# The first layer's high part of the weights times both parts of x in one product of 512 columns, from chunk 3 on

## The chip, the cores and the metric

The kernel runs on one core of a Trainium2 chip. The metric is the device time of one execution in microseconds (us). Engines are named as in the profile: PE multiplies matrices, PEld is its loading of the stationary operand, DVE is the vector engine, ACT the scalar engine, POOL the general engine, SP issues most transfers.

## The reference

Attention over 4 batches of 8 heads (768 positions, 64 wide) with a window of 128 positions and 4 sink positions, and then a feed-forward layer with a leaky activation on the 3072 resulting rows of width 512.

```python
scores = scale * np.matmul(q, k.transpose(0, 1, 3, 2))
keep = is_sink | in_window                      # 4 sinks, 128 positions back
a = softmax(np.where(keep, scores, -1e9))
x = np.matmul(a, v)                             # -> (3072, 512)
h = x @ w_in                                    # 512 -> 2048
g = np.maximum(h, 0.0) + alpha * np.minimum(h, 0.0)
out = g @ w_out                                 # 2048 -> 512, float32
```

## The kernel before

The 3072 rows are worked on in 12 chunks of 256 rows (`QC`), and the hidden width of 2048 in 16 blocks of 128 (`f`). PE multiplies in a reduced format, so a full product is made of three: each operand is split into a high part and the rest, and high x high, high x low and low x high are added up in PSUM. W_in and W_out of a block lie split in `fins[f]`, x of a chunk in `xh` and `xl` (a 128 x 4 x 256 tile each, two buffers each), and g in `gh` and `gl`.

A block (c, f) is `gemm1` and, two blocks later (`LAG`), `gemm2`. `gemm1` makes 12 products of 256 columns into one bank of the kind "h" (two such banks): for each of the four 128-row slices `kt` of x the high weights times `xh`, the high weights times `xl`, and the low weights times `xh` (L961). ACT then scales the bank by alpha into g (L977), DVE takes the larger of bank and g (L978), ACT rounds g to `gh` (L979), and DVE subtracts to get `gl` (L980). `gemm2` makes six products of 512 columns with them (L1034 and L1035 with `gh`, L1032 with `gl`) into the chunk's two output banks.

Beside the blocks of chunk c runs the attention of chunk c + 1: 16 units (8 heads, two halves of the queries). A unit is two score products on PE (L639, L640) into one of two banks of the kind "s", a masked sum with a maximum on DVE (L652), an exponential on ACT (L656), and scaling and combining on DVE (L686, L687, L698). For each pair of heads the weights are transposed through two transfers and masked on DVE (L780, L798 to L803). At the end `av_four` multiplies them by the values (L901, L914, L909), ACT rounds the result to `xh` (L946) and DVE subtracts to get `xl` (L947). Only then can the next chunk's first block start. Preparing a head's operands takes two DVE instructions (L605, L607); a further one (L441) looks through the weights for unusual exponents, in four blocks of a chunk.

Which step of the attention goes with which block is written down: the steps are spread over the first `SPAN` blocks of a chunk, and `av_four` goes with a later one:

```python
*most, last = attention(c + 1)
work += spread(most, SPAN) + [[] for _ in range(NF - SPAN)]
work[-3].append(last)
```

That order is only the rank of each operation. A list scheduler (`Plan.draw`) goes through all operations with a table of costs, takes for each engine the one that can start first (the lower rank among those nearly as early), and emits each engine's instructions in the order found; a set of nudges (`NUDGES`) moves the rank of some operations of chunks 0 to 2. What an engine's queue holds is therefore fixed before the run.

Of the kernel before, what the change touches and what calls it, by code (L numbers as in the profile page):

```python
# [48 lines left out]
SPAN = 12  # L49
# [23 lines left out]
WHOLE = 2  # L73
FIRST = 4
# [250 lines left out]
def cast(n, psum=False):  # L325
    return (0.045 if psum else 0.092) + 0.84e-3 * n
# [18 lines left out]
def mm(n):  # L345
    return 0.456e-3 * n
# [12 lines left out]
def program(ctx, tc, qk, qs, pairs, vp, vw, vq, vs, w, par, out):  # L359
# [33 lines left out]
    several("xh", 2, [P, KT, QC], F32R)  # L393
    several("xl", 2, [P, KT, QC], F32R)
# [194 lines left out]
    xh, xl, prep, comb, sink, ptile_, sums, rinv, nms, wt = {}, {}, {}, {}, {}, {}, {}, {}, {}, {}  # L589
# [233 lines left out]
    def begin_x(c, p):  # L823
        if p == 0:
            xh[c], xl[c] = val("xh"), val("xl")
        return xh[c], xl[c]

    def av_two(c, g):
# [11 lines left out]
        x1, x2 = begin_x(c, 2 * g)  # L840
        part = slice(2 * g, 2 * g + 2)
        keys = [[(t, x) for x in both] for t in (x1, x2)]
        view = lambda: bk.at.rearrange("p (n x) -> p n x", n=2)
        op("ACT", cast(4 * P, True), lambda: nc.scalar.copy(x1.at[:, part], view()), reads=[bk], writes=keys[0])
# [3 lines left out]
        op("DVE", dve(4 * P), lambda: nc.vector.tensor_tensor(x2.at[:, part], view(), x1.at[:, part].bitcast(F32), ALU.subtract),  # L848
           reads=[bk, *keys[0]], writes=keys[1])

    def av_split(c, g):
# [24 lines left out]
        x1, x2 = begin_x(c, 2 * g)  # L876
        part = slice(2 * g, 2 * g + 2)
        keys = [(x1, x) for x in both], [(x2, x) for x in both]
# [7 lines left out]
        op("ACT", cast(4 * P), lambda: nc.scalar.copy(x1.at[:, part], view()), reads=xs, writes=keys[0])  # L886
# [3 lines left out]
        op("DVE", dve(4 * P), lambda: nc.vector.tensor_tensor(x2.at[:, part], view(), x1.at[:, part].bitcast(F32), ALU.subtract),  # L890
           reads=[*xs, *keys[0]], writes=keys[1])

    def av_four(c):
# [11 lines left out]
        x1, x2 = begin_x(c, 0)  # L905
# [36 lines left out]
        for n, bk in enumerate(bks):  # L942
            part = slice(2 * n, 2 * n + 2)
            keys = [[(t, x) for x in range(2 * n, 2 * n + 2)] for t in (x1, x2)]
            view = lambda bk=bk: bk.at.rearrange("p (n x) -> p n x", n=2)
            op("ACT", cast(4 * P, True), lambda part=part, view=view: nc.scalar.copy(x1.at[:, part], view()), reads=[bk], writes=keys[0])  # L946
            op("DVE", dve(4 * P), lambda part=part, view=view: nc.vector.tensor_tensor(x2.at[:, part], view(), x1.at[:, part].bitcast(F32), ALU.subtract),  # L947
               reads=[bk, *keys[0]], writes=keys[1])
# [5 lines left out]
    def gemm1(c, f):  # L954
        bk, fin, x1, x2 = val("s" if c == NCHUNK - 1 and f >= NF - 2 else "h"), fins[f], xh[c], xl[c]
        h = lambda: bk.at[:, :QC]

        def some(kt):
            ks = slice(kt * P, (kt + 1) * P)
            for n, (part, rhs) in enumerate(((0, x1), (0, x2), (1, x1))):  # L960
                nc.tensor.matmul(h(), fin.at[:, 0, part, ks], rhs.at[:, kt], start=(kt == 0 and n == 0), stop=(kt == KT - 1 and n == 2))  # L961
# [12 lines left out]
        for kt in range(KT):  # L974
            op("PE", 3 * mm(QC), lambda kt=kt: some(kt), reads=[fin, (x1, kt), (x2, kt)], writes=[bk], tail=R_TAIL)
# [422 lines left out]
```

## Time and profile before

| | before |
|---|---|
| time, median of 3 runs | 655.55 us (655.27 to 655.95) |
| span of the profiled execution, first to last instruction | 653.5 us |
| PE busy | 646.0 us, 99% of the span |
| weight loads (PEld) busy | 577.5 us, 88% |
| DVE busy | 528.1 us, 81% |
| ACT busy | 387.0 us, 59% |
| granted PE clock | full in every slice |

The page of the profile gives the span of the profiled execution and not its whole time; the timed runs lie 1.8 to 2.4 us above that span, which is what comes before the first and after the last instruction. Busy time counts an instruction from its start to its end, and neighbours on one engine overlap: what an instruction takes away from its engine is read from start to start.

### The profile page before, as it was taken

How to read it: one execution, taken by the hardware profiler on the slowest of the kernel's cores; microseconds unless marked ns; L12 is line 12 of the kernel's file. 1: busy time of each engine (PE TensorE's matmuls, PEld its weight loads, DVE VectorE, ACT ScalarE, POOL GpSimd, SP SyncE). 2: the span in 40 equal slices, each digit the busy share in tenths (PEclk: the TensorE clock that was granted, in tenths of full speed). 3: DMA queues.
4: the chain of work that ended last, by engine and by line, in shares of the span. 5: the costliest groups of instructions: out<-in, count | busy, mean ns of one | idle time of the engine just before them, and what ended most of it. 6: DMA issues, size and time to landing. Idle time of an engine off the chain costs nothing.

```text
span 653.5 us, 14186 instructions
## 1 busy us (share of the span) xinstructions
PE 646.0 (99%) x4966; PEld 577.5 (88%) x4966; DVE 528.1 (81%) x1708; ACT 387.0 (59%) x1036; POOL 43.6 (7%) x139
## 2 busy tenths in 40 slices
PE   8999999999999999999999999999999999999997
PEld 4678988899999999999999999999999998998996
DVE  7999999987869959968968987986985995996332
ACT  6999667566456547638637736636645753753332
POOL 4100000010000001000000100001000000100000
PEclk9999999999999999999999999999999999999999
DMA  9996203743634646564563654574573564551001
GB/s 338 403 347 259 74 13 109 233 146 112 186 118 131 211 141 198 163 191 146 192 197 111 197 175 149 167 226 130 153 227 111 163 201 152 152 152 53 33 1 37
DMA packets 66508, 106.19 MB, mean 162 GB/s; under 512 B 10241, under 2 KB 33281, under 8 KB 66433
## 3 DMA queue, kind: packets, MB, share of 16 engines
q1 hardware_dynamic: 66144, 104.72, 49.7%
q8 instruction: 40, 0.66, 0.4%
q10 hardware_dynamic: 288, 0.53, 0.3%
q14 instruction: 36, 0.29, 0.2%
HBM read 87.14 MB, written 18.09 MB: 161 GB/s over the span
## 4 chain that ended last, share of the span: by engine, by line
PE 96%; ACT 1%; DVE 1%; DMA 0%; issue 0%; POOL 0%; SPq 0%; DVEq 0%
PE bank L961 40%; PE bank L1032 13%; PE bank L1034 13%; PE bank L1035 13%; PE bank L909 3%; PE bank L640 3%; PE bank L639 3%; PE bank L914 2%; PE bank L818 1%; PE bank L630 1%; PE bank L901 1%; ACT pt L656 1%; PE bank L965 1%; PE bank L994 1%; PE bank L677 0%; DMA param<-par 0%
## 5 line engine op out<-in xcount | busy, mean ns | idle before, releaser
L961 PE MATMUL bank<-xh,w 128*128 128x256 f32 x1520 | 300.5, 281 | 0.3 <-DVE g L978 0.2
L961 PEld LDWEIGHTS bank<-xh,w 128*128 128x128 f32 x1520 | 246.6, 189 | 5.7 <-DVE g L978 1.0
L961 PE MATMUL bank<-xl,w 128*128 128x256 f32 x760 | 212.3, 279 | 0.0
L1034 PE MATMUL bank<-w,gh 128*128 128x512 f32 (+1 forms) x390 | 150.3, 387 | 0.0
L977 ACT ACTIVATE g<-bank,param 128x256 f32<-128x256 f32 x190 | 89.6, 472 | 101.3 <-PE bank L961 93.7
L1035 PE MATMUL bank<-w,gh 128*128 128x512 f32 (+1 forms) x390 | 148.7, 385 | 0.0
L961 PEld LDWEIGHTS bank<-xl,w 128*128 128x128 f32 x760 | 143.3, 189 | 4.3
L979 ACT CAST gh<-g 128x256 fp32r<-128x256 f32 x190 | 77.2, 406 | 76.8 <-DVE g L978 75.9
L656 ACT ACTIVATE pt<-pt,nm 128x260 f32<-128x260 f32 (+1 forms) x192 | 94.5, 493 | 43.9 <-DVE nm L652 41.1
L978 DVE TENSOR_TENSOR g<-bank,g 128x256 f32<-128x256 f32 x190 | 79.6, 420 | 48.9 <-ACT g L977 47.1
L1032 PE MATMUL bank<-w,gl 128*128 128x512 f32 (+1 forms) x390 | 118.3, 388 | 0.0
L980 DVE TENSOR_TENSOR gl<-g,gh 128x256 fp32r<-128x256 f32 x190 | 79.5, 419 | 22.2 <-ACT gh L979 20.1
L652 DVE CUSTOM_DVE_ANT_0 pt<-bank,masks 128x260 f32<-128x260 f32 (+1 forms) x192 | 75.2, 401 | 14.4 <-PE bank L640 12.1
L1032 PEld LDWEIGHTS bank<-w,gl 128*128 128x128 f32 x390 | 70.7, 188 | 14.1 <-DVE gl L980 0.2
L1034 PEld LDWEIGHTS bank<-w,gh 128*128 128x128 f32 x390 | 73.4, 188 | 8.4
L1035 PEld LDWEIGHTS bank<-w,gh 128*128 128x128 f32 x390 | 73.4, 188 | 8.4
L702 POOL TENSOR_TENSOR sink<-pt,ri 128x8 f32<-128x8 f32 x80 | 23.7, 300 | 381.3 <-DVE ri L687 285.7
L605 DVE TENSOR_TENSOR kq<-stage,kq 64x392 fp32r<-64x392 f32 x80 | 45.1, 564 | 3.1
L640 PE MATMUL bank<-kq 128*128 128x260 f32 (+1 forms) x160 | 44.6, 281 | 0.0
L603 ACT CAST kq<-stage 128x392 fp32r<-128x392 f32 x80 | 41.1, 514 | 4.7 <-PE bank L640 3.4
L639 PE MATMUL bank<-kq 128*128 128x260 f32 (+1 forms) x160 | 43.7, 276 | 0.0
L698 DVE CUSTOM_DVE_ANT_0 comb<-pt,ri 128x128 f32<-128x128 f32 x136 | 43.2, 346 | 0.5
(141 smaller groups left out, 705.4 us busy)
## 6 DMA issues: line engine op xcount, KB each, us to landing
stage<-qs SPq DMA_DIRECT2D x80, 324.0 KB, 3.0
wraw<-w SPq DMA_DIRECT2D x16, 1024.0 KB, 9.0
wa<-w SPq DMA_DIRECT2D x32, 512.0 KB, 4.7
v<-vq SPq DMA_DIRECT2D x40, 256.0 KB, 3.7
swap<-comb SPq DMA_DIRECT2D x40, 256.0 KB, 2.2
comb<-swap SPq DMA_DIRECT2D x40, 256.0 KB, 3.4
out_dram<-ob SPq DMA_DIRECT2D x22, 256.0 KB, 3.5
stage<-pairs SPq DMA_DIRECT2D x4, 324.0 KB, 8.7
```

Of the source, the lines that this page charges most:

```text
L639: nc.tensor.matmul(s[:, w0], qh()[:, qs], ks()[:, kw], start=True, stop=False)
L640: nc.tensor.matmul(s[:, w0], ql()[:, qs], ks()[:, kw], start=False, stop=True)
L652: op("DVE", dve(n), lambda: nc.vector.tensor_tensor_reduce(out=pt.at[:, u, w0], in0=s.at[:, w0], in1=masks[:, i, w0], scale=-0.125, scalar ...
L656: op("ACT", exp(n), lambda: nc.scalar.activation(pt.at[:, u, w0], pt.at[:, u, w0], AF.Exp, bias=nm.at[:, h, u:u + 1], scale=-1.0, accum_ou ...
L961: nc.tensor.matmul(h(), fin.at[:, 0, part, ks], rhs.at[:, kt], start=(kt == 0 and n == 0), stop=(kt == KT - 1 and n == 2))
L977: op("ACT", act(QC, True), lambda: nc.scalar.activation(g.at, h(), AF.Copy, scale=alt[:, f:f + 1]), reads=[bk, known("param")], writes=[g])
L978: op("DVE", dve(QC), lambda: nc.vector.tensor_tensor(g.at, h(), g.at, ALU.max), reads=[bk], writes=[g])
L979: op("ACT", cast(QC), lambda: nc.scalar.copy(gh.at, g.at), reads=[g], writes=[gh])
L980: ending.append(op("DVE", dve(QC), lambda: nc.vector.tensor_tensor(gl.at, g.at, gh.at.bitcast(F32), ALU.subtract), reads=[g, gh], writes=[ ...
L1032: nc.tensor.matmul(to, gl.at[:, js], fin.at[:, 1, 0, cs], start=False, stop=(f == NF - 1))
L1034: nc.tensor.matmul(to, gh.at[:, js], fin.at[:, 1, 0, cs], start=(f == 0), stop=False)
L1035: nc.tensor.matmul(to, gh.at[:, js], fin.at[:, 1, 1, cs], start=False, stop=False)
```

## The change

From chunk 3 (`WIDE`) on, the high weights of a slice meet `xh` and `xl` in one product of 512 columns: the two parts of x lie in one tile, and the product fills the whole bank, its left half with high x high and its right half with high x low. The third product (low weights times the high part of x, 256 columns) is added to the left half. ACT then copies the right half to g instead of scaling the bank, DVE adds the left half to it, and a second DVE instruction multiplies by alpha and takes the larger value. So a block has 8 products instead of 12, as many columns as before, and one DVE instruction more. The attention's steps are spread over 11 blocks instead of 12, and `av_four` is ranked one block earlier. The edits of `av_two`, `av_split` and `av_four` only name the two parts of the one tile.

```diff
-SPAN = 12
+SPAN = 11
...
+WIDE = 3
...
-    several("xh", 2, [P, KT, QC], F32R)
-    several("xl", 2, [P, KT, QC], F32R)
+    several("x", 2, [P, 2, KT, QC], F32R)
...
     def begin_x(c, p):
         if p == 0:
-            xh[c], xl[c] = val("xh"), val("xl")
-        return xh[c], xl[c]
+            xs_of[c] = val("x")
+        return xs_of[c]
+
+    def x_keys(x, heads):
+        return [[(x, (n, h)) for h in heads] for n in range(2)]
...
     def gemm1(c, f):
-        bk, fin, x1, x2 = val("s" if c == NCHUNK - 1 and f >= NF - 2 else "h"), fins[f], xh[c], xl[c]
+        bk, fin, xx = val("s" if c == NCHUNK - 1 and f >= NF - 2 else "h"), fins[f], xs_of[c]
         h = lambda: bk.at[:, :QC]
+        wide = c >= WIDE
 
         def some(kt):
             ks = slice(kt * P, (kt + 1) * P)
-            for n, (part, rhs) in enumerate(((0, x1), (0, x2), (1, x1))):
-                nc.tensor.matmul(h(), fin.at[:, 0, part, ks], rhs.at[:, kt], start=(kt == 0 and n == 0), stop=(kt == KT - 1 and n == 2))
+            if wide:
+                nc.tensor.matmul(bk.at, fin.at[:, 0, 0, ks], xx.at[:, :, kt], start=kt == 0, stop=False)
+            else:
+                for n in range(2):
+                    nc.tensor.matmul(h(), fin.at[:, 0, 0, ks], xx.at[:, n, kt], start=kt == 0 and n == 0, stop=False)
+            nc.tensor.matmul(h(), fin.at[:, 0, 1, ks], xx.at[:, 0, kt], start=False, stop=kt == KT - 1)
...
         g, gh, gl = val("g"), val("gh"), val("gl")
-        op("ACT", act(QC, True), lambda: nc.scalar.activation(g.at, h(), AF.Copy, scale=alt[:, f:f + 1]), reads=[bk, known("param")], writes=[g])
-        op("DVE", dve(QC), lambda: nc.vector.tensor_tensor(g.at, h(), g.at, ALU.max), reads=[bk], writes=[g])
+        if wide:
+            op("ACT", act(QC, True), lambda: nc.scalar.copy(g.at, bk.at[:, QC:]), reads=[bk], writes=[g])
+            op("DVE", dve(QC), lambda: nc.vector.tensor_tensor(g.at, h(), g.at, ALU.add), reads=[bk], writes=[g])
+            op("DVE", dve(QC), lambda: nc.vector.scalar_tensor_tensor(g.at, g.at, alt[:, f:f + 1], g.at, op0=ALU.mult, op1=ALU.max), reads=[known("param")], writes=[g])
+        else:
+            op("ACT", act(QC, True), lambda: nc.scalar.activation(g.at, h(), AF.Copy, scale=alt[:, f:f + 1]), reads=[bk, known("param")], writes=[g])
+            op("DVE", dve(QC), lambda: nc.vector.tensor_tensor(g.at, h(), g.at, ALU.max), reads=[bk], writes=[g])
...
         work += spread(most, SPAN) + [[] for _ in range(NF - SPAN)]
-        work[-3].append(last)
+        work[-4].append(last)
```

In what follows a row is an engine's instruction: line, operation, the tiles it writes and reads, and the columns. In the change the lines move: L961 becomes L965 (wide) and L969 (narrow), L1034, L1035 and L1032 become L1047, L1048 and L1045, L901 becomes L904, L947 becomes L950, L978 becomes L987 and L988, L980 becomes L993.

PE before, at the end of chunk 6, where the values of chunk 7 are made (`w_1032` is block 14, `w_961` block 12, `w_895` block 11):

```order
L961 MATMUL bank_69<-xh_116,w_1032 128x256 x2
L961 MATMUL bank_69<-xl_118,w_1032 128x256
L961 MATMUL bank_69<-xh_116,w_1032 128x256
L1034 MATMUL bank_70<-w_961,gh_124 128x512
L1035 MATMUL bank_70<-w_961,gh_124 128x512
L1034 MATMUL bank_71<-w_961,gh_124 128x512
L1035 MATMUL bank_71<-w_961,gh_124 128x512
L901 MATMUL bank_66<-sinkT_112,vs_113 128x256 x2
L901 MATMUL bank_67<-sinkT_112,vs_113 128x256 x2
```

PE in the change, at the same place (`w_992` is block 13, `w_1030` block 14; block 15's last first-layer product stands four rows ahead of the first of these):

```order
L1045 MATMUL bank_70<-w_992,gl_124 128x512
L1045 MATMUL bank_71<-w_992,gl_124 128x512
L1047 MATMUL bank_70<-w_1030,gh_120 128x512
L1048 MATMUL bank_70<-w_1030,gh_120 128x512
L1047 MATMUL bank_71<-w_1030,gh_120 128x512
L1048 MATMUL bank_71<-w_1030,gh_120 128x512
L639 MATMUL bank_65<-kq_80 128x260
L640 MATMUL bank_65<-kq_80 128x260
L639 MATMUL bank_64<-kq_80 128x260
L640 MATMUL bank_64<-kq_80 128x260
L904 MATMUL bank_66<-sinkT_112,vs_113 128x256 x2
L904 MATMUL bank_67<-sinkT_112,vs_113 128x256 x2
```

Before, the values stand between block 14's products and block 15's; now all of block 15's first-layer products, and the second layer of blocks 13 and 14, stand ahead of them, and two units of the next attention's scores as well. In the eight chunks that prepare another one with the new products (3 to 10) the values stand after block 15's first-layer products in seven and in the middle of block 15's in one; before, they stand next to block 14's in all eight.

DVE before, at the start of chunk 7, from the subtraction that completes x on:

```order
L947 TENSOR_TENSOR xl_119<-bank_67,xh_117 128x512
L978 TENSOR_TENSOR g_121<-bank_68,g_121 128x256
L980 TENSOR_TENSOR gl_125<-g_121,gh_124 128x256
L978 TENSOR_TENSOR g_120<-bank_69,g_120 128x256
L980 TENSOR_TENSOR gl_126<-g_120,gh_123 128x256
L652 ISA pt_86,nm_100<-bank_65,masks 128x260
L652 ISA nm_100 128x1
L652 ISA pt_86,nm_100<-bank_64,masks 128x260
L652 ISA nm_100 128x1
L978 TENSOR_TENSOR g_121<-bank_68,g_121 128x256
L605 TENSOR_TENSOR kq_80<-stage_78,kq_80 64x392
L607 TENSOR_TENSOR kq_80<-stage_78,kq_80 128x256
```

DVE in the change, at the same place, after the same subtraction (now L950):

```order
L652 ISA pt_88,nm_100<-bank_65,masks 128x260
L652 ISA nm_100 128x1
L652 ISA pt_88,nm_100<-bank_64,masks 128x260
L652 ISA nm_100 128x1
L698 ISA comb_93,jk_110<-pt_86,ri_104 128x128
L698 ISA jk_110 128x1
L698 ISA comb_93,jk_108<-pt_86,ri_104 128x128
L698 ISA jk_108 128x1
L605 TENSOR_TENSOR kq_81<-stage_79,kq_81 64x392
L607 TENSOR_TENSOR kq_81<-stage_79,kq_81 128x256
L987 TENSOR_TENSOR g_118<-bank_69,g_118 128x256
L988 SCALAR_TENSOR_TENSOR g_118<-g_118,param 128x256
```

The work of two units of the next attention now stands ahead of the first block's activation, and that activation has become a pair, L987 and L988, of which the second reads what the first writes.

## Rows read from the trace of the kernel before

**Rows 1.** The page: header, and busy time, share of the span and instructions by engine.

```profile
span 653.5 us, 14186 instructions
...
PE 646.0 (99%) x4966; PEld 577.5 (88%) x4966; DVE 528.1 (81%) x1708; ACT 387.0 (59%) x1036; POOL 43.6 (7%) x139
```

**Rows 2.** The chain that ended last, share of the span by engine.

```profile
PE 96%; ACT 1%; DVE 1%; DMA 0%; issue 0%; POOL 0%; SPq 0%; DVEq 0%
```

**Rows 3.** What PE waited for, whole run: total us, times, longest.

```profile
PE bank L1192 <- DVE fm L585: 1.1, 1, 1.1
...
PE bank L961 <- DVE g L978: 0.2, 1, 0.2
```

**Rows 4.** Busy time by windows, values to values: the sum of seven periods.

```profile
sum 362.30, PE 362.30 PEld 330.81 DVE 299.91 ACT 207.72 POOL 23.39; mean PE 51.76 PEld 47.26 DVE 42.84 ACT 29.67 POOL 3.34
```

**Rows 5.** One period in two windows: from:to us, PE, PEld, DVE, ACT, POOL busy.

```profile
386.70:398.00 11.30, 11.30 (x153) 10.25 (x152) 5.54 (x13) 3.65 (x9) 0.85 (x2) 1.00 0.44 148
398.00:438.70 40.70, 40.70 (x271) 37.23 (x270) 38.31 (x138) 26.36 (x77) 2.58 (x8) 1.00 0.60 180
```

**Rows 6.** Timeline of PE: start us, duration, line, operation, tiles, columns, count.

```profile
340.27 0.39 PE L1034 MATMUL bank<-w,gh 128*128 128x512 f32 x1
...
341.18 0.62 PE L1032 MATMUL bank<-w,gl 128*128 128x512 f32 x2
...
343.03 0.40 PE L1034 MATMUL bank<-w,gh 128*128 128x512 f32 x1
...
343.97 0.62 PE L1032 MATMUL bank<-w,gl 128*128 128x512 f32 x2
...
396.72 0.28 PE L961 MATMUL bank<-xh,w 128*128 128x256 f32 x1
...
398.09 0.28 PE L639 MATMUL bank<-kq 128*128 128x260 f32 x1
...
436.37 0.28 PE L961 MATMUL bank<-xh,w 128*128 128x256 f32 x1
...
437.78 0.39 PE L1034 MATMUL bank<-w,gh 128*128 128x512 f32 x1
```

**Rows 7.** Timeline of DVE.

```profile
357.80 0.43 DVE L980 TENSOR_TENSOR gl<-g,gh 128x256 fp32r<-128x256 f32 x1
358.14 0.42 DVE L607 TENSOR_TENSOR kq<-stage,kq 128x256 fp32r<-128x256 f32 x1
...
433.00 0.68 DVE L798 TENSOR_TENSOR comb<-comb,tri 128x512 f32<-128x512 f32 x1
433.72 0.69 DVE L800 TENSOR_TENSOR comb<-comb,tri 128x512 f32<-128x512 f32 x1
```

**Rows 8.** Groups by line and shape: xcount, busy us, mean ns, idle before.

```profile
L441 DVE SCALAR_TENSOR_TENSOR odd<-wa,odd 128x512 int32<-128x512 int32 x32 | 22.0, 688 | 11.2 <-DMA wa<-w 11.2
...
L947 DVE TENSOR_TENSOR xl<-bank,xh 128x512 fp32r<-128x512 f32 x20 | 12.9, 686 | 8.0 <-ACT xh L946 8.0
```

**Rows 9.** Timeline around the values of chunk 8: scores, masking, values, x.

```profile
396.48 0.28 PE L639 MATMUL bank<-kq 128*128 128x260 f32 x1
...
436.92 0.69 DVE L800 TENSOR_TENSOR comb<-comb,tri 128x512 f32<-128x512 f32 x1
...
438.70 0.63 PE L901 MATMUL bank<-sinkT,vs 128*128 128x256 f32 x4
...
442.42 0.74 PE L1032 MATMUL bank<-w,gl 128*128 128x512 f32 x2
...
443.18 1.29 DVE L947 TENSOR_TENSOR xl<-bank,xh 128x512 fp32r<-128x512 f32 x2 [0.68 <-ACT xh L946]
```

**Rows 10.** Timeline of the last chunk: from a block's last product to its freed bank.

```profile
641.92 0.28 PE L961 MATMUL bank<-xh,w 128*128 128x256 f32 x1
...
642.29 0.47 ACT L977 ACTIVATE g<-bank,param 128x256 f32<-128x256 f32 x1 [1.44 <-PE bank L961]
...
642.80 0.42 DVE L978 TENSOR_TENSOR g<-bank,g 128x256 f32<-128x256 f32 x1 [1.49 <-ACT g L977]
```

More of the change, by code (lines that the diff above doesn't have):

```diff
@@ L839, in av_two @@
         op("PE", 2 * mm(QC) + 2 * values_cost(c), run, reads=[vt, st, *src, *v], writes=[bk], tail=N_TAIL, mode="col")
-        x1, x2 = begin_x(c, 2 * g)
+        xx = begin_x(c, 2 * g)
         part = slice(2 * g, 2 * g + 2)
-        keys = [[(t, x) for x in both] for t in (x1, x2)]
+        keys = x_keys(xx, both)
         view = lambda: bk.at.rearrange("p (n x) -> p n x", n=2)
-        op("ACT", cast(4 * P, True), lambda: nc.scalar.copy(x1.at[:, part], view()), reads=[bk], writes=keys[0])
+        op("ACT", cast(4 * P, True), lambda: nc.scalar.copy(xx.at[:, 0, part], view()), reads=[bk], writes=keys[0])
         if not g:
@@ L847, in av_two @@
                 load_v(c, x + 2)
-        op("DVE", dve(4 * P), lambda: nc.vector.tensor_tensor(x2.at[:, part], view(), x1.at[:, part].bitcast(F32), ALU.subtract),
+        op("DVE", dve(4 * P), lambda: nc.vector.tensor_tensor(xx.at[:, 1, part], view(), xx.at[:, 0, part].bitcast(F32), ALU.subtract),
            reads=[bk, *keys[0]], writes=keys[1])
@@ L875, in av_split @@
         op("PE", 2 * values_cost(c), both_values, reads=[t for two in src for t in two] + v, writes=[bk], tail=N_TAIL, mode="col")
-        x1, x2 = begin_x(c, 2 * g)
+        xx = begin_x(c, 2 * g)
         part = slice(2 * g, 2 * g + 2)
-        keys = [(x1, x) for x in both], [(x2, x) for x in both]
+        keys = x_keys(xx, both)
         if c:
@@ L885, in av_split @@
                reads=[bk, rb], writes=xs)
-        op("ACT", cast(4 * P), lambda: nc.scalar.copy(x1.at[:, part], view()), reads=xs, writes=keys[0])
+        op("ACT", cast(4 * P), lambda: nc.scalar.copy(xx.at[:, 0, part], view()), reads=xs, writes=keys[0])
         if c and not g:
@@ L889, in av_split @@
                 load_v(c, x + 2)
-        op("DVE", dve(4 * P), lambda: nc.vector.tensor_tensor(x2.at[:, part], view(), x1.at[:, part].bitcast(F32), ALU.subtract),
+        op("DVE", dve(4 * P), lambda: nc.vector.tensor_tensor(xx.at[:, 1, part], view(), xx.at[:, 0, part].bitcast(F32), ALU.subtract),
            reads=[*xs, *keys[0]], writes=keys[1])
@@ L904, in av_four @@
         v = [vtile.pop((c, x)) for x in every]
-        x1, x2 = begin_x(c, 0)
+        xx = begin_x(c, 0)
         def whole(x, u):
@@ L943, in av_four @@
             part = slice(2 * n, 2 * n + 2)
-            keys = [[(t, x) for x in range(2 * n, 2 * n + 2)] for t in (x1, x2)]
+            keys = x_keys(xx, range(2 * n, 2 * n + 2))
             view = lambda bk=bk: bk.at.rearrange("p (n x) -> p n x", n=2)
-            op("ACT", cast(4 * P, True), lambda part=part, view=view: nc.scalar.copy(x1.at[:, part], view()), reads=[bk], writes=keys[0])
-            op("DVE", dve(4 * P), lambda part=part, view=view: nc.vector.tensor_tensor(x2.at[:, part], view(), x1.at[:, part].bitcast(F32), ALU.subtract),
+            op("ACT", cast(4 * P, True), lambda part=part, view=view: nc.scalar.copy(xx.at[:, 0, part], view()), reads=[bk], writes=keys[0])
+            op("DVE", dve(4 * P), lambda part=part, view=view: nc.vector.tensor_tensor(xx.at[:, 1, part], view(), xx.at[:, 0, part].bitcast(F32), ALU.subtract),
                reads=[bk, *keys[0]], writes=keys[1])
```

4 lines of the change are left out of this document (2 added, 2 removed).

## Prediction

> **What bounds the kernel now.** I read the page's busy shares first: PE is busy for 99% of 653.5 us, its weight loads for 88%, DVE for 81%, ACT for 59% [rows 1]. A busy PE alone proves little, since its products overlap, so the chain that ended last comes next: 96% of it is PE [rows 2]. The third view is what PE waited for: four waits in the whole run, the longest 1.1 us and the shortest 0.2 us, 3.0 us together [rows 3]. So time can only be won by making PE's own queue shorter, and any wait that PE is given is lost.
>
> The engine that could give it one is DVE. From one chunk's values to the next, seven periods take 362.30 us with PE busy throughout and DVE for 299.91 us [rows 4]: 51.8 us a period, DVE 42.8, so 8.9 us free. One period taken apart shows where the free time lies. In the 11.3 us after the values of chunk 7 DVE is busy for 5.54 us, in the next 40.7 us for 38.31, or 94% [rows 5]. In that second part DVE sets the pace of the attention: the last masking starts at 436.92 and takes 0.69 us, and the values of chunk 8 start 1.1 us after it ends [rows 9]. They wait for DVE already; PE does not notice because it has blocks 14 and 15 to put beside them.
>
> **PE's columns.** In chunks 3 to 11 there are 9 x 16 x 4 = 576 pairs of narrow products that become one wide product each. The columns stay the same; only what a product costs beyond its columns can be saved. I read that from start to start. Twelve narrow products take 1.37 us in one block and 1.41 us in another, 0.114 and 0.1175 us each; four wide products of the second layer take 0.91 and 0.94 us, 0.2275 and 0.235 us each [rows 6]. Fast against fast, a pair costs 0.2283 and a wide product 0.2275; slow against slow, 0.235 and 0.235. The saving is 0 to 0.8 ns a pair; I take 0.5 ns, so **0.3 us** in all. PE's rate has these two levels in stretches of a block, for no reason that the rows show, and the new order might shift their mix. If all 144 new blocks ran at the fast one (4 x (0.2275 + 0.114) = 1.366 us) against a mean of 1.39, that is 144 x 0.023 = 3.3 us less; all at the slow one (1.41 us) 2.9 us more.
>
> The loads deserve a sentence of rows, since 576 of 4966 go. They overlap the products, and where one load goes with 512 columns instead of 256 (the second layer) a column takes as long: 0.2275/512 and 0.114/256 us are both 0.44 ns [rows 6]. Loads do not set the pace. The Trainium skill, in Trainium Kernel Development and Optimization (Best Practices), says to judge the distance to the bound by the share of weight loads rather than by busy products; by that rule the 88% are the number to bring down, and the change does so. TensorE: Matmul & The Clock Gate (LDWEIGHTS) puts a load of 128 columns at 107 ns, as long as a narrow product's stream, and Back-to-back issue gap a lone wide product at 216 ns; as an estimate from that page, a pair at 232 ns would then save 16 ns, or 9 us in all. The trace disagrees, since its wide products, with loads to spare, are at 227 to 235 ns.
>
> **DVE's added instruction.** Each of 144 blocks gets an L988 of 256 elements with three inputs. No row shows one of this shape; its nearest are L441, the same operation at 512 elements, with 688 ns, and a two-input operation at 512, L947, with 686 ns [rows 8]. So it costs what a two-input one of 256 does: 0.34 us from start to start when the next does not depend on it. An instruction that reads what the one before it writes starts later: the pair L798 and L800 stand 0.72 us apart at 0.68 us of duration [rows 7], while independent ones overlap by 0.09 us (0.43 us long, 0.34 apart). The order puts L988 right behind L987 in most places, so a block gives up 0.34 to 0.45 us of DVE; I take 0.45, the row it is nearest to. A period has 16 blocks: 7.2 us of the 8.9 us free. It fits, barely, if almost no other idle time is left.
>
> ACT's copy replaces ACT's scaling, same size, and ACT is at 59%: nothing. Merging the two parts of x into one tile moves no instruction.
>
> **Where the shortage shows.** Blocks themselves are safe: `gemm2` runs two blocks later, and DVE gives up attention work first. So the attention comes late, at the values. From the first scores at 396.48 to the values at 438.70 [rows 9] lie about 13 blocks, so 13 x 0.45 = 5.9 us more DVE work. What covers that? First, the place. The order has moved the values from between blocks 14 and 15 to behind block 15's first layer, so PE does the following ahead of them that stood behind them before: the rest of block 12 (two wide products, 0.46 us), block 15's first layer (1.39), the second layer of block 13 (six wide, 1.38) and four products of block 14 (0.92): 4.15 us. Second, an earlier start: the order has two units' scores in front of the values and their DVE work ahead of the first activation, where DVE had 11.3 - 5.54 = 5.8 us free; three blocks' own 1.35 us must come off, so up to 4.4 us. Late by 5.9 - 4.15 - (0 to 4.4): between 2.65 us early and 1.75 us late, at each of 8 boundaries. The order itself says that it is close: where the values stand, PE has no first-layer work of the old chunk left.
>
> What is late next: behind the values in PE's queue stand the second layer of block 15 and the new chunk's first products. Those need x, 0.76 us until L947 starts after the values leave PE and 0.69 us for its first half, 1.45 us [rows 8, 9]; the queue has 1.4 to 2.3 us of other work there, so this costs 0 to 0.1 us. Then in five of eight boundaries three first layers follow each other, and the third needs the first one's bank. Its last product starts at 641.92 in the last chunk, ACT at 642.29, and DVE's reading ends at 642.80 + 0.42 = 643.22, with an idle DVE [rows 10]; the product itself leaves about 0.116 us after its start, so 1.18 us, against 1.39 us of the second first layer. A busy DVE (0.1 to 0.6 us for whatever it is in) turns the 0.2 us of slack into 0 to 0.4 us of waiting. I take 0.25 us a boundary for all of this, near the lower end, because DVE's sum over a period still fits: **2.0 us**.
>
> **The sum.** The profiled execution: 653.5 - 0.3 + 2.0 = 655.2 us of span. The median stands 2.05 us above that span before, and I keep that: **657.2 us**, 0.26% more than 655.55. About 0.2% (1.3 us) is what a measurement of this kernel can tell from no change, so faster means under 654.2 and slower over 656.9.
>
> **The rivals.**
> - *DVE overfull.* If the earlier start yields nothing, each boundary is 1.75 us late: 655.55 - 0.3 + 14 = 669 us; half of it gives 662. For it: 7.2 of 8.9 us free, and idle time that can't be filled, such as that before x. Against it: two units do stand earlier. It decides from the point where DVE's idle time in a period falls under some 1.5 us. Chance 0.17.
> - *Nothing is lost.* The earlier start and the place cover everything: 655.2 us, the same. For it: PE waited 3.0 us in all before, with an attention as tight. Against it: the values' place behind the last first layer. Chance 0.16.
> - *PE gains, the other side.* The first layer settles at the fast rate with half as many loads of its high weights, and DVE keeps up: 655.55 - 0.3 - 3.3 = 652.0 us. For it: the fast rate exists in whole blocks. Against it: second-layer products are wide and no faster. By the estimate from the Trainium skill's page above it would be 646. Chance 0.17.
>
> The forecast itself has 0.5, from 655.2 to 659.5; a bit over half of that lies above 656.9. So slower: 0.26 + 0.17 + 0.04 (a slow mix of rates with nothing else lost) = 0.47; same: 0.24 + 0.10 = 0.34; faster: 0.17 + 0.02 = 0.19. The range of 8 in 10 leaves out the upper half of the first rival and the lower half of the third: 652.5 to 664.0 us. The forecast's own range is 655.2 to 659.5.
>
> **What would show it.** PE has 4390 products, 576 of them L965; from a first L965 to the eighth product's end a block takes 1.37 to 1.41 us. L988 has 144 instructions of about 420 ns, and DVE's busy time is near 528 + 144 x 0.42 = 588 us. The list of PE's waits has new lines at the values (L904, L917) on L801 or L803, or at L965 on L950 and L987, one or two at each boundary and 2 us together. The forecast is wrong if blocks take clearly under 1.36 us, if waits appear inside a chunk (L1047 on `gh`, L1045 on `gl`), which would mean that DVE puts the attention ahead of the blocks, or if the waits at the boundaries exceed 1 us each.

## The result: 1.0% slower

| | before | after |
|---|---|---|
| time, median | 655.72 us (655.27 to 655.95, 4 runs) | 662.37 us (661.44 to 663.02, 4 runs) |
| span of the profiled execution | 653.5 us | 659.7 us |

The ratio is 1.0102, with a 95% interval of 1.0090 to 1.0115. The direction and the range of 8 in 10 (652.5 to 664.0 us) hold. The forecast's own range, 655.2 to 659.5, was missed: its 657.2 us had a quarter of the loss (1.65 us where 6.65 came). A second set of runs of the change gave 661.99 us.

The page of the changed kernel, header and engines (compare [rows 1]):

```profile
span 659.7 us, 13066 instructions
...
PE 650.7 (99%) x4389; PEld 553.3 (84%) x4390; DVE 587.2 (89%) x1852; ACT 370.8 (56%) x1036; POOL 46.9 (7%) x139
```

PE is still busy for 99%, and that line alone would hide the loss. The share of weight loads fell from 88% to 84%, DVE's rose from 81% to 89%. The chain that ended last says more (compare [rows 2]):

```profile
PE 85%; DVE 10%; ACT 2%; issue 1%; DMA 0%; POOL 0%; DVEq 0%; SPq 0%; ACTq 0%
```

PE held 96% of it before and DVE 1%. What PE waited for, total us, times, longest (compare [rows 3]):

```profile
PE bank L1205 <- DVE fm L585: 1.1, 1, 1.1
PE bank L751 <- DVE ts L733: 0.9, 1, 0.9
PE bank L639 <- DVE nm L652: 0.8, 2, 0.5
PE bank L965 <- DVE g L987: 0.4, 1, 0.4
PE bank L968 <- DVE g L991: 0.2, 1, 0.2
```

New are the third line, scores that wait until a masking has read their bank, and the fourth, a block's first product that waits until L987 has read its bank. That list counts only the time in which no product is in flight. The list of what the weight loads waited for, which stand ahead of the products, shows the same two releasers with more:

```profile
PEld bank L639 <- DVE nm L652: 3.0, 6, 0.8
...
PEld bank L965 <- DVE g L987: 1.4, 2, 0.8
```

DVE from values to values, seven periods in one line (compare [rows 4]):

```profile
sum 367.96, PE 366.66 PEld 312.68 DVE 345.74 ACT 195.84 POOL 26.50; mean PE 52.38 PEld 44.67 DVE 49.39 ACT 27.98 POOL 3.79
```

The periods take 5.7 us more together. DVE is busy for 49.39 us of 52.57, so 3.2 us are free in one, where 8.9 were.

The groups of the two instructions that replace the former comparison (compare [rows 8]):

```profile
L987 DVE TENSOR_TENSOR g<-bank,g 128x256 f32<-128x256 f32 x144 | 59.8, 416 | 16.4 <-ACT g L986 15.8
L988 DVE SCALAR_TENSOR_TENSOR g<-g,param 128x256 f32<-128x256 f32 x144 | 70.1, 487 | 3.8
```

Two more things are read from starts. On DVE, L987, L988 and an instruction that needs neither (compare [rows 7]):

```profile
273.68 0.42 DVE L987 TENSOR_TENSOR g<-bank,g 128x256 f32<-128x256 f32 x1
274.13 0.49 DVE L988 SCALAR_TENSOR_TENSOR g<-g,param 128x256 f32<-128x256 f32 x1
274.53 0.42 DVE L652 CUSTOM_DVE_ANT_0 pt<-bank,masks 128x260 f32<-128x260 f32 x1
```

L988 holds the engine for 0.40 us, and it starts 0.45 us after L987 where an independent instruction would start after 0.34: 0.51 us a block. On PE, one whole block (compare [rows 6]):

```profile
274.10 0.39 PE L965 MATMUL bank<-x,w 128*128 128x512 f32 x1
274.33 0.28 PE L969 MATMUL bank<-x,w 128*128 128x256 f32 x1
274.45 0.40 PE L965 MATMUL bank<-x,w 128*128 128x512 f32 x1
274.68 0.28 PE L969 MATMUL bank<-x,w 128*128 128x256 f32 x1
...
275.15 0.40 PE L965 MATMUL bank<-x,w 128*128 128x512 f32 x1
275.39 0.28 PE L969 MATMUL bank<-x,w 128*128 128x256 f32 x1
275.51 0.39 PE L1047 MATMUL bank<-w,gh 128*128 128x512 f32 x1
```

1.41 us, with 0.23 to 0.24 for each wide product and 0.11 to 0.12 for each narrow one. A block of before that stands at nearly the same time (its twelve products begin with the first row, the sixth with the second):

```profile
272.51 0.28 PE L961 MATMUL bank<-xh,w 128*128 128x256 f32 x1
...
273.11 0.39 PE L961 MATMUL bank<-xh,w 128*128 128x256 f32 x2
...
273.90 0.39 PE L1034 MATMUL bank<-w,gh 128*128 128x512 f32 x1
```

The first five products, behind the wide ones of a second layer, take 0.60 us, 0.12 each; the other seven take 0.79 us, 0.113 each. There the narrow products came down to the fast rate; in the block of the change, where the widths take turns, they don't.

To compare whole runs I took every product from chunk 3 on (of 256, 260 or 512 columns, without the values) and the time from its start to the next one's start. What that has beyond 116, 120 or 231 ns counts as a wait where it is over 25 ns, and as rate otherwise. "Block" is the mean of the blocks whose products stand together and that take under 1.45 us, so that waits stay out.

```
                                          time      span    waits   rate   block
before                                    655.72    653.5   1.90   -0.02   1.395 us
the change                                662.37    659.7   4.99    2.87   1.409
```

Waits have 3.1 us more and the rate 2.9 us. The last product starts 4.6 us ahead of the span's end before and 5.3 us after, 0.7 us more; other products give 0.5 us back. That makes the 6.2 us of span. Waits are those of one profiled execution: the second profile of the change has 6.19 us of them, 1.2 more, at one place (shown further down), so a difference of about 1 us in this column says little.

### The profile page after: what moved, and what is told of

Same layout as the page of the kernel before. It is cut to its first block, busy times and chain, and to the rows that moved or that the text cites. A ratio compares the mean times of both kernels' runs of the same rounds, so it can differ in the third digit from the quotient of the medians.

```text
span 659.7 us, 13066 instructions
## 1 busy us (share of the span) xinstructions
PE 650.7 (99%) x4389; PEld 553.3 (84%) x4390; DVE 587.2 (89%) x1852; ACT 370.8 (56%) x1036; POOL 46.9 (7%) x139
## 4 chain that ended last, share of the span: by engine, by line
PE 85%; DVE 10%; ACT 2%; issue 1%; DMA 0%; POOL 0%; DVEq 0%; SPq 0%; ACTq 0%
PE bank L965 18%; PE bank L1045 12%; PE bank L969 12%; PE bank L1047 12%; PE bank L1048 11%; PE bank L968 5%; PE bank L912 3%; PE bank L639 2%; PE bank L640 2%; PE bank L917 2%; DVE kq L605 1%; DVE pt L652 1%; DVE g L988 1%; DVE comb L698 1%; DVE kq L607 1%
## 5 line engine op out<-in xcount | busy, mean ns | idle before, releaser
L969 PE MATMUL bank<-x,w 128*128 128x256 f32 x760 | 213.1, 280 | 0.0
L965 PE MATMUL bank<-x,w 128*128 128x512 f32 x576 | 209.6, 397 | 0.5 <-DVE g L987 0.4
L1047 PE MATMUL bank<-w,gh 128*128 128x512 f32 (+1 forms) x390 | 150.4, 387 | 0.0
L1048 PE MATMUL bank<-w,gh 128*128 128x512 f32 (+1 forms) x390 | 148.6, 384 | 0.0
L969 PEld LDWEIGHTS bank<-x,w 128*128 128x128 f32 x760 | 143.0, 188 | 3.0
L965 PEld LDWEIGHTS bank<-x,w 128*128 128x128 f32 x576 | 108.2, 188 | 24.1 <-DVE g L987 1.4
L1045 PE MATMUL bank<-w,gl 128*128 128x512 f32 (+1 forms) x390 | 118.5, 388 | 0.0
L986 ACT COPY g<-bank 128x256 f32<-128x256 f32 x144 | 53.2, 370 | 78.1 <-PE bank L969 70.3
L993 DVE TENSOR_TENSOR gl<-g,gh 128x256 fp32r<-128x256 f32 x190 | 79.4, 419 | 13.3 <-ACT gh L992 10.8
L1047 PEld LDWEIGHTS bank<-w,gh 128*128 128x128 f32 x390 | 73.3, 188 | 13.1 <-ACT ob L1053 0.2
L1045 PEld LDWEIGHTS bank<-w,gl 128*128 128x128 f32 x390 | 69.9, 188 | 13.3
L1048 PEld LDWEIGHTS bank<-w,gh 128*128 128x128 f32 x390 | 73.4, 188 | 8.9
L987 DVE TENSOR_TENSOR g<-bank,g 128x256 f32<-128x256 f32 x144 | 59.8, 416 | 16.4 <-ACT g L986 15.8
L988 DVE SCALAR_TENSOR_TENSOR g<-g,param 128x256 f32<-128x256 f32 x144 | 70.1, 487 | 3.8
L968 PE MATMUL bank<-x,w 128*128 128x256 f32 x368 | 68.3, 283 | 0.4 <-DVE g L991 0.2
L968 PEld LDWEIGHTS bank<-x,w 128*128 128x128 f32 x368 | 58.5, 188 | 4.5 <-DVE g L991 1.0
L603 ACT CAST kq<-stage 128x392 fp32r<-128x392 f32 x80 | 41.5, 519 | 11.8 <-PE bank L640 10.9
```

Of the source, the lines that this page charges most:

```text
L965: nc.tensor.matmul(bk.at, fin.at[:, 0, 0, ks], xx.at[:, :, kt], start=kt == 0, stop=False)
L968: nc.tensor.matmul(h(), fin.at[:, 0, 0, ks], xx.at[:, n, kt], start=kt == 0 and n == 0, stop=False)
L969: nc.tensor.matmul(h(), fin.at[:, 0, 1, ks], xx.at[:, 0, kt], start=False, stop=kt == KT - 1)
L988: op("DVE", dve(QC), lambda: nc.vector.scalar_tensor_tensor(g.at, g.at, alt[:, f:f + 1], g.at, op0=ALU.mult, op1=ALU.max), reads=[known("p ...
L993: ending.append(op("DVE", dve(QC), lambda: nc.vector.tensor_tensor(gl.at, g.at, gh.at.bitcast(F32), ALU.subtract), reads=[g, gh], writes=[ ...
L1045: nc.tensor.matmul(to, gl.at[:, js], fin.at[:, 1, 0, cs], start=False, stop=(f == NF - 1))
```

## Experiments

**Theories.** 1: the instruction added on DVE makes PE wait for banks. 2: wide and narrow products in turn keep PE at the slower of its two rates, whatever DVE does. 3, the rival: the order (`SPAN`, the place of `av_four`) costs by itself. The first three kernels keep these two ranks of the change and add its two other parts singly. Ranks are not queues, though: the scheduler draws the queues anew for each kernel. In the traces, DVE's instructions and PE's blocks, scores and values stand in the order of the change only in the second of the three. In the first and the third, 15 first-layer blocks of the chunk stand ahead of the values (14 at two of the eight boundaries), as before; in the change there are 16 (15 and a half at one).

**The order alone.**

```diff
-WIDE = 3
+WIDE = NCHUNK
```

> Only the order of the change is kept (attention over 11 blocks, values a block sooner, the two parts of x in one tile); the first layer of all chunks has its three narrow products and its single comparison on VectorE as before. Theory 1 (the instruction added on VectorE makes TensorE wait) and theory 2 (a wide product followed by a narrow one runs at the slower of TensorE's two rates) both expect the time of before: 655.7 us, within 0.7 us, with four waits of TensorE of about 3 us together. Theory 3 (the place of the values and the shorter attention cost by themselves) expects 657.5 to 661 us, with waits at the values or at the first products behind them.

656.29 us, ratio 1.0014 (1.0005 to 1.0023): 0.8 us over its own runs of before. Waits are those of before (1.87 us by the reckoning above). But the values stand where they stood before, as the first product of chunk 7's values shows, here (first row) and in the change (second row):

```profile
387.04 0.63 PE L904 MATMUL bank<-sinkT,vs 128*128 128x256 f32 x4
394.76 0.63 PE L904 MATMUL bank<-sinkT,vs 128*128 128x256 f32 x4
```

Before, it starts at 386.66. So the ranks alone do not move the values: the scheduler puts them behind block 15 only when it has the second DVE instruction to place. This kernel does not test theory 3 for the queues of the change, and no kernel here has those queues without that instruction. The 0.8 us lie in the rate: 0.4 us in products of the first layer and 0.2 us in those of the second, whose inputs and number the order leaves as they were.

**The added DVE instruction alone.**

```diff
         def some(kt):
...
-            if wide:
+            if False:
...
-            op("ACT", act(QC, True), lambda: nc.scalar.copy(g.at, bk.at[:, QC:]), reads=[bk], writes=[g])
-            op("DVE", dve(QC), lambda: nc.vector.tensor_tensor(g.at, h(), g.at, ALU.add), reads=[bk], writes=[g])
+            op("ACT", act(QC, True), lambda: nc.scalar.copy(g.at, h()), reads=[bk], writes=[g])
+            op("DVE", dve(QC), lambda: nc.vector.tensor_tensor(g.at, h(), g.at, ALU.max), reads=[bk], writes=[g])
```

> The order of the change, narrow products as before, but chunks 3 to 11 get the second VectorE instruction of the change: ScalarE only copies, VectorE takes a maximum of the sum with its own copy and then the scaled comparison L988, 144 instructions more, the output unchanged. Theory 1 expects most of the loss here: 658 to 660 us, TensorE waiting for score banks (L639 on L652) and for first-layer banks (the first product of a block on L987), about 2 to 3 us more of waiting than before. Theory 2 expects the time of before, 655.7 us within 0.7. If both are at work and add up, about 659.

660.67 us, ratio 1.0078 (1.0064 to 1.0092): 4.4 us over the order alone, a little above what theory 1 had. The queues are those of the change, so the 4.4 us hold the instruction together with the queues that the scheduler draws for it; the two are not separated. PE's waits in this kernel:

```profile
PE bank L968 <- DVE g L987: 1.4, 2, 0.9
PE bank L639 <- DVE nm L652: 1.1, 3, 0.5
```

The waits of over 0.25 us stand where those of the change stand, with narrow products here and wide ones there, in chunks 3, 4, 6 and 10; one more, of 1.1 us in chunk 5, the second profile of the change has too, and one of 0.35 us in chunk 9 is this kernel's own. Blocks stay at 1.397 us, as with the order alone: no loss of rate.

**The wide products alone.**

```diff
-        if wide:
+        if False:
             op("ACT", act(QC, True), lambda: nc.scalar.copy(g.at, bk.at[:, QC:]), reads=[bk], writes=[g])
```

> The order of the change and its 576 wide products, but VectorE has the single comparison of before; left out is the right half of the bank, so the product of W_in's high part and x's low part is computed and not added to the rest. Theory 2 expects a block of 1.41 us in place of 1.40 and so about 2 us more than before, 657.2 to 658.5 us, without new waits. Theory 1 alone expects the time of before, 655.7 us within 0.7. If wide products are as fast as two narrow ones, blocks stay at 1.40 us.

657.92 us, ratio 1.0041 (1.0027 to 1.0054): 1.6 us over the order alone. Waits as before (1.95 us); a block takes 1.408 us in place of the 1.397 of the order alone, and 0.011 us in 144 blocks is 1.6 us. Theory 2 holds without DVE's part. PE's and DVE's queues are the same here as with the order alone, so nothing else differs between the two. The change and the DVE instruction alone are such a pair too, in the other queues, and differ by 1.3 to 1.7 us. Order 0.8, DVE 4.4 and wide products 1.6 make 6.8 us; the change lost 6.65 and, the second time, 6.4. So the parts add up, with the new queues counted under DVE.

**Does the layout of x slow the wide products?** The kernel before this one, with the two parts of a slice of x side by side:

```diff
-    several("x", 2, [P, 2, KT, QC], F32R)
+    several("x", 2, [P, KT, 2, QC], F32R)
...
-                nc.tensor.matmul(bk.at, fin.at[:, 0, 0, ks], xx.at[:, :, kt], start=kt == 0, stop=False)
+                nc.tensor.matmul(bk.at, fin.at[:, 0, 0, ks], xx.at[:, kt], start=kt == 0, stop=False)
```

> As the run with wide products and one VectorE comparison (left out again: the product of W_in's high part and x's low part is computed and not added), but x is laid out so that the 512 elements of a wide product stand side by side; before, its two halves of 256 stood 4 KB apart. If reading two pieces is what keeps the wide products at 235 ns, they come down to about 231 ns, blocks to 1.40 us, and the time to that of the order alone, 656.3 us within 0.6. If the layout has no part in it, the time stays at 657.9, within 0.6, and the products at 234 to 235 ns.

657.76 us, ratio 1.0035 (1.0021 to 1.0049), a block 1.408 us. The layout has no part in it.

**Or the turns of width?** All of the change, four wide products of a block first, then its four narrow ones:

```diff
-        for kt in range(KT):
-            op("PE", 3 * mm(QC), lambda kt=kt: some(kt), reads=[fin, (xx, (0, kt)), (xx, (1, kt))], writes=[bk], tail=R_TAIL)
+        if wide:
+            for part, cost in ((high, 4), (low, 2)):
+                for k in (0, 2):
+                    op("PE", cost * mm(QC), lambda part=part, k=k: pair(part, k),
+                       reads=[fin] + [(xx, (n, x)) for n in range(2) for x in (k, k + 1)], writes=[bk], tail=R_TAIL)
...
```

> All of the change, with the eight products of a block in another order: first the four wide ones, then the four narrow ones, instead of wide and narrow in turn. If it is the turn from wide to narrow that keeps a block at the slower rate (theory 2 in its strict form), some blocks go at the faster one and the time is 1 to 3 us under that of the change, 659.5 to 661.5 us, the waits staying. If the rate does not hang on the neighbours, a block takes 1.41 us as in the change and the time stays at 662.4, within 0.7. Theory 1 expects 662.4 too.

663.42 us, ratio 1.0124 (1.0108 to 1.0139), not the gain that theory 2's strict form expected. The rate did come down (1.3 us instead of 2.9, the middle block at 1.395 instead of 1.409 us), but the waits grew from 5.0 to 7.7 us: the order of all engines had moved with it. So I took DVE's part out of it, by the same edit as in the run with wide products alone:

> Wide products with VectorE's single comparison (left out: the product of W_in's high part and x's low part is computed and not added), the four wide products of a block first and the four narrow ones behind them. If the turns between wide and narrow products hold a block at 1.409 us, a block takes 1.39 us here and the time is 1.5 to 2.5 us under that of the ungrouped one (657.9): 655.4 to 656.4 us, without new waits. If the grouping itself made the full change slower (663.4 against 662.4), by something other than VectorE's waits, it is 658.5 us or more.

657.34 us, ratio 1.0030 (1.0021 to 1.0039), between the two cases. PE's blocks, scores and values stand as in the ungrouped one, and waits are as before (1.85 us). A block, four wide products and four narrow ones by starts:

```profile
272.76 1.09 PE L983 MATMUL bank<-x,w 128*128 128x512 f32 x4
273.69 0.64 PE L986 MATMUL bank<-x,w 128*128 128x256 f32 x4
274.16 0.40 PE L1062 MATMUL bank<-w,gh 128*128 128x512 f32 x1
```

0.93 and 0.47 us, 1.40 together. The mean block is 1.401 us against 1.408 in turn and 1.397 narrow. By the rate of the first layer's products, the wide products cost 2.0 us in turn and 1.2 us grouped: grouping gives back about half of what the blocks had lost, most of it in the narrow products. The time shows 0.6 us of it (the intervals overlap), and the rate of all products 0.4 us, so other products became slower by some. So the turns are a part of the cause in the block; what makes up the rest stays open.

**Half of the DVE instructions.** As the DVE part alone, but in even blocks only:

```diff
-        wide = c >= WIDE
+        wide = c >= WIDE and f % 2 == 0
```

> As the run with the second VectorE instruction on narrow products, output unchanged, but only in the even blocks of chunks 3 to 11: 72 added instructions instead of 144. If the loss is a shortage that begins when VectorE's free time in a period is used up (a period has some 9 us free, 72 instructions take 4 us of it, 144 take 8), half of them cost little: 656.3 to 657.3 us, without waits on L652 or L987. If each added instruction costs by itself (its block ends later and something waits for it each time), half of them cost half: 658.5 us, within 0.6.

658.31 us, ratio 1.0046 (1.0032 to 1.0060): half the instructions, about half the loss, as if each cost by itself. The trace says otherwise. Waits are 1.6 us above those of the order alone, and all of that lies in one place, 397.8 to 403.3 us, where the scores behind the values of chunk 7 wait for maskings; it also holds the only new lines of the list for scores:

```profile
PE bank L639 <- DVE nm L652: 0.7, 2, 0.4
```

So in this kernel it is neither the same price for each instruction nor a threshold for a whole period: one stretch of DVE's queue overflows and the others do not. Its queues are drawn anew as well (they are neither those of the change nor those of the order alone), so where the full stretches lie is its own.

**The place taken back.** All of the change but this:

```diff
-SPAN = 11
+SPAN = 12
...
-        work[-4].append(last)
+        work[-3].append(last)
```

> All of the change except its place: attention over 12 blocks and the last step in the block where it was, as before. If the earlier attention covers a part of VectorE's shortage, as the prediction has it (4 us of TensorE's work a boundary, part of it needed), taking it back costs: 663.5 to 675 us, with waits at the values or behind them. If the place only has its own small cost (the order alone was 0.8 us over before), the time is 661.6 us, within 0.7.

668.52 us, ratio 1.0208 (1.0194 to 1.0222): 6.2 us slower than the change. Its waits:

```profile
PE bank L639 <- DVE nm L652: 3.8, 7, 0.8
PE bank L965 <- DVE x L950: 1.7, 3, 0.8
```

The second line is the wait for x, which the change does not have. In the queues that came of it the values do not go back to where they stood before: all of block 15's first layer stands ahead of them at all eight boundaries, and at four of them more of the second layer than in the change. What was taken back is the earlier attention, and it was worth 6.2 us. All waits of over 0.15 us lie between 2.8 us ahead of the values and 10.9 us behind them, where the prediction had looked for them.

**The subtraction moved to POOL.** All of the change, and for blocks 0 to 13:

```diff
-        ending.append(op("DVE", dve(QC), lambda: nc.vector.tensor_tensor(gl.at, g.at, gh.at.bitcast(F32), ALU.subtract), reads=[g, gh], writes=[gl]))
+        less = lambda e: e.tensor_tensor(gl.at, g.at, gh.at.bitcast(F32), ALU.subtract)
+        by = ("POOL", pool2(QC), lambda: less(nc.gpsimd)) if wide and f < NF - 2 else ("DVE", dve(QC), lambda: less(nc.vector))
+        ending.append(op(*by, reads=[g, gh], writes=[gl]))
```

> All of the change, the output unchanged, but for blocks 0 to 13 of chunks 3 to 11 the subtraction that makes gl goes from VectorE to GpSimd, 126 instructions; VectorE so has about the load of before. Theory 1 (VectorE's load makes TensorE wait; 4.4 us in the run with the added instruction alone) expects the waits on L652 and L987 to go and 657.4 to 659 us, the time of the run with wide products alone. A rival expects no gain or a loss, 661 us or more: GpSimd's subtraction takes longer and VectorE's instructions are stretched beside it, or the second layer waits for gl.

677.52 us, ratio 1.0338 (1.0324 to 1.0352): the rival, by far. PE's waits:

```profile
PE bank L904 <- DMA sinkT<-turns: 5.0, 5, 1.2
PE bank L639 <- DVE nm L652: 4.7, 11, 0.6
```

The group of the moved instruction on POOL:

```profile
L993 POOL TENSOR_TENSOR gl<-g,gh 128x256 fp32r<-128x256 f32 x126 | 97.9, 777 | 283.7 <-ACT gh L992 163.9 <-issue 72.5 <-PE bank L969 26.4
```

And the group of a DVE instruction that runs beside it:

```profile
L698 DVE CUSTOM_DVE_ANT_0 comb<-pt,ri 128x128 f32<-128x128 f32 x136 | 60.7, 470 | 0.5
```

POOL takes 777 ns where DVE took 419, and L698 on DVE, 345 to 347 ns in the other kernels, takes 470. With both inputs in SBUF it is stretched: 53 of the 136 meet no work on POOL and keep 346 ns, the other 83 take 549 ns on average. L987, which has one input in PSUM, stays at 415 ns. The Trainium skill says so in GPSIMD Engine Reference (Key points): the two engines share their SBUF interfaces, with contention for DVE instructions of two SBUF inputs. The trace agrees. The values also wait for the sinks' transfer, five times, which no other kernel here shows; whether POOL's queue or the new order (the values stand ahead of block 15's first layer again) made it late was not taken apart.

**The change again**, beside the last kernel.

> The change itself once more, beside the other run: 662.4 us within 0.6, and a block of its first layer at 1.409 us.

661.99 us, ratio 1.0093 (1.0078 to 1.0109), a block 1.409 us, waits 6.2 us, rate 2.8 us. The waits are those of the first profile and one more, of 1.0 us, at the third first layer behind the values of chunk 5:

```profile
297.68 1.29 POOL L510 TENSOR_TENSOR vs<-ob,vs 64x512 fp32r<-64x512 f32 x1 [3.27 <-issue]
297.95 1.57 DVE L441 SCALAR_TENSOR_TENSOR odd<-wa,odd 128x512 int32<-128x512 int32 x1 [0.22 <-DMA wa<-w]
299.91 0.50 PE L965 MATMUL bank<-x,w 128*128 128x512 f32 x1 [0.84 <-DVE g L987]
```

L441 had waited for a transfer, met POOL's instruction and took 1.57 us instead of 0.69, and L987, which frees PE's bank, stands behind it. In the first profile L441 starts at 297.61, just ahead of POOL, and keeps its 0.69 us; there it is L988 that is stretched, to 1.06 us, and PE does not wait for it.

All of them by the same reckoning, from the profiled executions:

```
                                          time      span    waits   rate   block
the order alone                           656.29    654.6   1.87    0.78   1.397 us
+ DVE instruction in even blocks          658.31    656.8   3.48    1.03   1.398
+ DVE instruction                         660.67    659.9   6.99    0.57   1.397
+ wide products                           657.92    656.2   1.95    2.65   1.408
+ wide products, x side by side           657.76    656.0   1.90    2.68   1.408
+ wide products, grouped                  657.34    655.6   1.85    2.29   1.401
the change again                          661.99    660.8   6.19    2.80   1.409
the change, grouped                       663.42    661.4   7.73    1.29   -
the change, old place                     668.52    666.4  11.49    2.50   1.407
the change, gl on POOL                    677.52    674.8  18.82    2.70   1.409
```

## Why the prediction was right, and where its sizes were off

**PE bounds it, and any wait is lost: right.** In each kernel of the table the waits and the rate move the time by about as much.

**PE's columns: the term that failed outright.** It was to be 0.3 us of gain; the wide products cost 1.6 us (runs alone), and the change's trace has 2.9 us of rate where that of before has none. The prediction priced a pair against a wide product at either rate, rightly, and then kept the mix of rates, "for no reason that the rows show". The trace of before did hold one: narrow products behind wide ones start at 0.12 us and may come down to 0.113 (by their place in the block, the first four stand 117 to 118 ns apart and the sixth to the eleventh 115 on average). In 32% of the blocks before the twelve take under 1.385 us; with wide and narrow in turn 3% do. All blocks at the slow rate was the upper bound of this term, 1.41 us a block, and that case came. The share of weight loads fell from 88% to 84%. The Trainium skill (Trainium Kernel Development and Optimization, Best Practices) has the distance to the bound judged by that share, together with the share of the peak arithmetic that is used (MFU). By that, a lower share means more distance; the prediction took it for something to aim at. In this trace the share alone does not tell the distance: it fell because 576 loads are gone, PE stayed busy for 99%, and the run with wide products alone lost 1.6 us.

**DVE's added instruction: too cheap.** 0.51 us instead of 0.45, because L988 takes 487 ns and not 420, and holds its engine for 0.40 us. 16 x 0.51 = 8.2 of 8.9 us. DVE's busy time came out as forecast (587.2 against 588), since busy time leaves the overlaps out.

**Where the shortage shows: right cause, wrong place, half the size.** The forecast had it at the values and behind them, 0.25 us a boundary, 2.0 us in all. From the change's 144 instructions, with the queues drawn for them, come 4.4 us. The values are never waited for, nor x: the place and the earlier attention do cover that, as the prediction said, and the kernel without the earlier attention loses 6.2 us more, near the rival of an overfull DVE (669 us). The prediction put the later place of the values down to the change of ranks; the order alone shows that the ranks do not move them. What was left out stands in the middle of a period. PE has two banks for scores and two for first layers, and DVE frees them in its fixed order. So waits did appear inside a chunk, as the prediction's signs of being wrong had it, though on other lines. The timeline of both engines in the change at its longest wait, in chunk 4:

```profile
262.56 0.56 DVE L605 TENSOR_TENSOR kq<-stage,kq 64x392 fp32r<-64x392 f32 x1
...
263.15 0.42 DVE L607 TENSOR_TENSOR kq<-stage,kq 128x256 fp32r<-128x256 f32 x1
...
264.04 0.42 DVE L987 TENSOR_TENSOR g<-bank,g 128x256 f32<-128x256 f32 x1
...
264.49 0.49 DVE L988 SCALAR_TENSOR_TENSOR g<-g,param 128x256 f32<-128x256 f32 x1
264.64 0.28 PE L969 MATMUL bank<-x,w 128*128 128x256 f32 x1
264.89 0.42 DVE L652 CUSTOM_DVE_ANT_0 pt<-bank,masks 128x260 f32<-128x260 f32 x1
...
265.24 0.42 DVE L652 CUSTOM_DVE_ANT_0 pt<-bank,masks 128x260 f32<-128x260 f32 x1
...
265.38 0.39 PE L639 MATMUL bank<-kq 128*128 128x260 f32 x1 [0.47 <-DVE nm L652]
```

DVE goes from one instruction to the next without a gap. PE has issued its product at 264.64 and could go on 0.12 us later with scores, but their bank is read by the first of the two maskings, which stand behind the pair L987 and L988; scores start at 265.38, 0.63 us late. Such places, for banks of scores, are at 210.5, 264.6 and 578.3 us, all near block 8 of a chunk, and hold 0.40, 0.73 and 0.57 us. With 1.07 us for banks of the first layer, at 383.7 to 387.2 us, they make 2.8 of the 3.1 us of new waits.

**The bank of the first layer: priced at 0 to 0.4 us a boundary.** In the first profile it is not waited for behind the values, where the prediction had it, but twice ahead of them, at blocks 13 and 14 of chunk 6, 11 and 8 us before chunk 7's values. The first time:

```profile
382.83 0.21 DVE L732 CAST ts<-sink 128x128 fp32r<-128x128 f32 x1
...
383.08 0.29 DVE L733 TENSOR_TENSOR ts<-sink,ts 128x128 fp32r<-128x128 f32 x1
...
383.40 0.45 DVE L740 STREAM_TRANSPOSE pt<-ts 128x256 f32<-128x256 f32 x1
...
383.77 0.39 DVE L987 TENSOR_TENSOR g<-bank,g 128x256 f32<-128x256 f32 x1
...
384.21 0.19 PEld L965 LDWEIGHTS bank<-x,w 128*128 128x128 f32 x1 [0.56 <-DVE g L987]
```

ACT had copied by 383.17 (not shown), but three instructions for the sinks stood in front of L987. The place that the prediction named, the third first layer behind the values, shows its wait only in the second profile (1.0 us) and in the DVE instruction alone (1.1 us), at one boundary of eight.

**Blocks themselves are safe: right for the second layer.** Nothing waits for `gh` or `gl`.

**The rivals.** "Nothing is lost" and "PE gains" did not come; for the latter the rate moved the other way. The overfull DVE is what the old place shows. The prediction had half of that rival at 662 us, the time that came, but by waits at the boundaries, which hold almost nothing of it. The range reaches up to 664 us because of that rival, so that it holds is partly luck: 1.6 us came from a term that was to be a gain, and most of the rest from places that the sum had left out.

**What stays open:** why the order alone slows PE's products by 0.8 us in all, why some narrow blocks come down to the fast rate and others not, and how much of DVE's 4.4 us is the instruction and how much the queues that were drawn for it. No kernel here beats the one before: wide products without DVE's second instruction are slower too (657.34 us at best), so taking load off DVE would not by itself have made the change pay.

## What to carry to other kernels

Merging products saves nothing where PE's time goes with the columns, and it can cost: read start to start what the products beside them do, not only the merged ones. An engine with 8.9 us free in a period of 51.8 had no room here for 8.2 us more, because it also hands banks back: ask for each bank what stands in front of the instruction that frees it, in the middle of a period as well as at its end. Moving work to an idle engine needs the same look at what it shares with the full one. And where a scheduler draws the queues, a kernel with one part taken out can differ in more than that part: read the queues from its trace before comparing times.

## What the hardware showed that I had not expected

- The rate of PE at a full clock depends on the neighbours: narrow products beside wide ones at 117 to 118 ns, in a run of their own often at 113 to 114; wide ones mostly at 232 to 235 ns in turn with narrow ones and at 226 to 237 in the second layer.
- A three-input DVE instruction of 256 elements with a scalar from SBUF takes 487 ns, one of two inputs 416 (L988 and L987 of the change); at 512 elements the two stood at 688, on integers, and 686 [rows 8].
- POOL's subtraction of 256 elements takes 777 ns and stretches a DVE instruction with two SBUF inputs from 345 to 470 ns on average; which of two DVE instructions meets POOL can change from one execution to the next.
